# Turning x of a head pair through a scratch in DRAM: four transfers out and one back in place of sixteen

## The chip, the core and the metric

The kernel runs on one core of one Trainium2 chip. The metric is the device time of one execution in microseconds, taken as the median of several runs; beside it there is one profiled execution with a record of the instructions of each engine, of the DMA issues with their landings, and of the clock granted to TensorE (PE).

## The reference

The input is q, k, v of shape (8 batches, 8 heads, 576 positions, 64), all float32, a norm weight g, and the weights of a mixer. The first half is linear attention without a softmax, with an RMS norm over each head's 64 outputs; the second half mixes along the sequence with a rank-32 product and then runs a two-layer network along the channels:

```python
kv = np.einsum('bhsd,bhde->bhse', q, np.einsum('bhsd,bhse->bhde', k, v))   # out
x = out / sqrt(mean(out * out, -1) + 1e-6) * g_norm       # heads side by side: (8, 576, 512)
u = x + (x.transpose(0, 2, 1) @ U @ V).transpose(0, 2, 1)
y = u + np.maximum(u @ w_ch1, 0) @ w_ch2                  # 512 -> 2048 -> 512
```

## The kernel before, in words

**The network.** The 8 x 576 = 4608 positions are cut into nine blocks of 512 columns, j = 0 to 8. The kernel keeps u with channels on the partitions, in two parts (a rounded high part and the rest, so a product takes three matmuls). Blocks 0 and 1 go through all 16 chunks of the hidden size with `ffn1` (L454 to L456, accumulating in the tile h), `relu` (ACT L463 makes hh, DVE L464 makes hl) and `ffn2` (L471, accumulating in y). From block 2 on, `fast_group` takes two chunks at a time by a scheme of seven products instead of eight (L607, into h and pp in turn); DVE and ACT add the products up (L666, L662), make hh and hl (L669, L670), and the matmuls of L625 bring them into y. There are 8 groups a block and 7 such blocks. This is called the fast stage below; it starts at 246 us.

**Weights.** They come as 64-bit words, are decoded on ACT and DVE during block 0, and during block 1 `weight_combos` forms the sums for the seven products on POOL, DVE (L568, L572) and ACT (L570), in tiles named dec and sh. L574 to L577 store them in DRAM tiles wd, one for each of the 8 groups. In the fast stage `load_group` (L597) brings each group's weights back in two loads, wt<-wd, 1024 and 768 KB, into one of two buffer sets; a load waits until PE has finished with the buffer.

**The pairs.** Heads are taken in pairs, four pairs a batch. A pair of batch b is prepared while an earlier block runs: batch 0 before block 0, batch 1 in block 0, batch 2 in block 1, and batches 3 to 7 in the fast stage, so that 28 of the 32 pairs go the way described here and 20 of these in the fast stage. The steps: `kv_step` (PE L274 to L281, after loads of kv_sb and kvt_sb, DVE L272 and L288), `out_step` (PE L300, L302, after the load of q_sb; ACT squares), `stats_step` and `mul_step` (DVE L316 to L331: the norm, giving x with positions on the partitions), `xsplit_step`, `turn_step`, `t_step` and `t4_step` (the rank-32 product), and `mix_part` (PE L440, then DVE L443 adds the turned x). `carry` (ACT L515), `split_cols` and `factor` (L543 to L548) make the network's operands of it.

**The turn.** `turn_step` brings x, positions on the partitions, into ut32[p], channels on the partitions. DVE transposes 32 x 32 squares (L356) into xt; what is left is to move squares between groups of 32 partitions. L359 does it with sixteen transfers, SBUF to SBUF, one for each source group a and target group k, 20 KB each for a = 0 and 1, and 16 KB for a = 2 and 3. The mix of the pair, L443, needs all sixteen.

**The order.** All transfers are issued by SP, one queue, in order; an instruction that waits holds all behind it. SP issues the loads of the pairs and the weights, the turns, the stores of the weight sums and of the output (out<-st, L487). PE's order in the fast stage is written out by hand: the pair steps are put behind numbered products. The order of DVE, ACT, POOL and SP, and PE's in blocks 0 and 1, comes from a scheduler which places each instruction when it takes its operands to be ready; so an instruction's new cost can change the order around it.

Of the kernel before, what the change touches and what calls it, by code (L numbers as in the profile page):

```python
# [10 lines left out]
F32 = mybir.dt.float32  # L11
# [8 lines left out]
B, H, S, D = 8, 8, 576, 64  # L20
DM, DF, R = 512, 2048, 32
P = 128
# [9 lines left out]
QL = [P + 32] * 2 + [P] * 2  # L32
QO = [0, 160, 320, 448]
# [40 lines left out]
def build(ctx: ExitStack, tc: tile.TileContext, kv_in, kvt0_in, kvt_in, q_in, uv_in, g_in, w_in, out):  # L74
    nc = tc.nc
# [14 lines left out]
    ut32 = [ut32_all[:, c, :] for c in range(ND)]  # L90
# [165 lines left out]
    def bank():  # L256
        bank_no[0] += 1
        if startup[0] and bank_no[0] % (7 - NEARLY) >= 3 - NEARLY:
            return ps_y.tile([P, 512], F32, name="y")
        return ps_p.tile([P, 512], F32, name="pp")  # L260
# [73 lines left out]
    def xsplit_step(b, p):  # L334
# [9 lines left out]
        nc.vector.tensor_tensor(out=xh[TAIL:P, 4], in0=s["x"][0:TAIL, 4], in1=xh[0:TAIL, 4].bitcast(F32), op=ALU.subtract)  # L344
        s["hl"] = (xh, xl)

    def turn_step(b, p):

        x = state[b, p]["x"]
        if b == 0:  # L350
            main = state[b, p]["main"] = bank()
            for i in range(4):
                nc.tensor.matmul(main[:, i * P:(i + 1) * P], lhsT=x[:, i, :], rhs=ident, start=(i == 0), stop=False, is_transpose=True)
        else:
            xt = sc.tile([P, 4, NT, 32], F32, name="xt")
            nc.vector.transpose(out=xt.rearrange("p k i j -> p i k j"), in_=x.rearrange("p i (k j) -> p i k j", j=32))  # L356
            for a in range(4):
                for k in range(4):
                    nc.sync.dma_start(out=ut32[p][32 * k:32 * k + 32, QO[a]:QO[a] + QL[a]],  # L359
                                      in_=xt[32 * a:32 * a + 32, k, 0:QL[a] // 32].rearrange("p i j -> p (i j)"))  # L360

    def t_step(b, p):
        tp = bank()
# [414 lines left out]
    def spread_v(n, eng):  # L778
# [4 lines left out]
        out=uv, in_=uvraw.bitcast(U32).rearrange("p (n t) -> p n t", t=2)[:, :, 1].bitcast(F32), func=AF.Abs)  # L783
# [122 lines left out]
    def pair_steps(b, p):  # L906

        nxt = (b, p + 1) if p + 1 < NPAIR else (b + 1, 0)

        def kv():  # L910
            kv_step(b, p)
            if nxt[0] < B:
                load_kv(*nxt)

        def o():
            for what in (out_step, stats_step, mul_step):
                what(b, p)
            if nxt[0] < B:
                load_q(*nxt)

        def t():
            t_step(b, p)
            t4_step(b, p)

        return dict(kv=kv, out=o, carry=lambda: carry(b, p), turn=lambda: turn_step(b, p), xsplit=lambda: xsplit_step(b, p), t=t, mix0=lambda: mix_part(b, p, 0), mix1=lambda: mix_part(b, p, 1))
# [141 lines left out]
```

## Time and profile before

| what | us |
|---|---|
| median of 3 runs | 909.07 (908.11 to 911.46) |
| profiled execution | 908.89 |
| its span | 907.1 |
| PE busy in the span | 888.4 |
| SP: 448 issues of L359, median | 0.588 each |
| DVE at L443 idle for ut<-xt | 17.4, 12 times |

The span runs from the first to the last instruction; 1.79 us of the profiled execution lie around it. A row of a timeline or a group gives, in square brackets, how long the engine stood idle ahead of it and what ended that. A row of SP gives the time in which it issued a number of transfers; the transfers land later.

### The profile page before, as it was taken

The page shows a single profiled execution, that of the slowest core. Times are in us where ns is not written, and L with a number is a line of the kernel's source. Part 1 is how long each engine was busy: PE and PEld are TensorE (multiplying, and loading weights), DVE is VectorE, ACT ScalarE, POOL GpSimd, SP SyncE. Part 2 cuts the span into 40 slices and gives each one's busy share as a digit, 9 for nine tenths or more (in the row PEclk, how much of TensorE's full clock was granted, in tenths as well). Part 3 has the DMA queues.
Part 4 walks back from the last instruction along what each step waited for, and adds up shares of the span by engine and source line. Part 5 has one row for each costly group of instructions (what it writes and reads, how often), then busy time and mean ns, then how long its engine had stood idle before and what let it go on. Part 6 is the DMA issues. An engine that isn't in the chain of part 4 may idle for free.

```text
span 907.1 us, 15333 instructions
## 1 busy us (share of the span) xinstructions
PE 888.4 (98%) x5540; PEld 788.2 (87%) x5540; DVE 569.8 (63%) x1278; ACT 368.3 (41%) x818; POOL 38.0 (4%) x53
## 2 busy tenths in 40 slices
PE   8899999999999999999999999999999999999997
PEld 7678888887889998899999999999999999998997
DVE  5799987668475577566856586558755662253233
ACT  5677743333244353444533354335332432232221
POOL 2000023212010000000000000000000000000000
PEclk9999999999999999999999999999999999999999
DMA  9966355544756565666665557557744665546541
GB/s 345 417 263 195 101 182 158 182 147 155 268 184 243 223 245 166 229 239 216 221 220 224 183 189 257 179 213 259 262 168 174 215 221 186 163 163 213 180 142 47
DMA packets 76541, 186.81 MB, mean 206 GB/s; under 512 B 12721, under 2 KB 45233, under 8 KB 69297
## 3 DMA queue, kind: packets, MB, share of 16 engines
q1 hardware_dynamic: 76464, 185.82, 58.3%
q8 instruction: 44, 0.72, 0.3%
q14 instruction: 33, 0.26, 0.1%
HBM read 149.73 MB, written 24.12 MB: 192 GB/s over the span
## 4 chain that ended last, share of the span: by engine, by line
PE 82%; DMA 7%; DVE 4%; SPq 3%; ACT 2%; issue 1%; POOL 0%; DVEq 0%; ACTq 0%
PE y L625 31%; PE h L607 15%; PE pp L607 14%; PE y L471 6%; SPq L359 3%; PE h L454 2%; PE pp L277 2%; PE h L455 2%; PE pp L300 2%; PE h L456 2%; DMA out<-st 1%; DMA wt<-wd 1%; DMA wd<-dec 1%; DMA ut<-xt 1%; DMA kvq<-kv_in 1%
## 5 line engine op out<-in xcount | busy, mean ns | idle before, releaser
L607 PE MATMUL h<-uc,wt 128*128 128x256 f32 x1176 | 175.2, 285 | 0.3 <-DVE sums L666 0.3
L625 PE MATMUL y<-hh,ws 128*128 128x512 f32 (+1 forms) x528 | 175.1, 389 | 0.0
L607 PE MATMUL pp<-uc,wt 128*128 128x256 f32 x1176 | 173.1, 283 | 0.1
L607 PEld LDWEIGHTS h<-uc,wt 128*128 128x128 f32 x1176 | 161.2, 190 | 10.2 <-DVE sums L666 0.7
L607 PEld LDWEIGHTS pp<-uc,wt 128*128 128x128 f32 x1176 | 154.9, 191 | 0.5 <-DVE sums L666 0.3
L625 PEld LDWEIGHTS y<-hh,ws 128*128 128x128 f32 x528 | 97.5, 189 | 16.2
L625 PE MATMUL y<-dec,ws 128*128 128x512 f32 (+1 forms) x396 | 103.0, 389 | 0.0
L625 PE MATMUL y<-hl,ws 128*128 128x512 f32 (+1 forms) x264 | 102.8, 389 | 0.0
L666 DVE TENSOR_TENSOR sums<-h,dec 128x256 f32<-128x256 f32 x112 | 47.1, 421 | 64.1 <-PE h L607 63.3
L625 PEld LDWEIGHTS y<-dec,ws 128*128 128x128 f32 x396 | 70.3, 189 | 11.9
L669 ACT ACTIVATE hh<-sums 128x512 fp32r<-128x512 f32 x75 | 47.0, 629 | 80.3 <-DVE sums L666 78.7
L666 DVE TENSOR_TENSOR sums<-pp,dec 128x256 f32<-128x256 f32 x112 | 47.1, 421 | 46.0 <-PE pp L607 39.8
L471 PE MATMUL y<-hh,ws 128*128 128x512 f32 x216 | 71.6, 397 | 0.2 <-ACT hh L463 0.2
L662 ACT COPY dec<-h 128x256 f32<-128x256 f32 x84 | 31.2, 372 | 86.2 <-PE h L607 85.9
L670 DVE SCALAR_TENSOR_TENSOR hl<-sums,hh 128x512 fp32r<-128x512 f32 x75 | 51.9, 692 | 18.9 <-ACT hh L669 18.2
L625 PEld LDWEIGHTS y<-hl,ws 128*128 128x128 f32 x264 | 49.9, 189 | 7.6
L454 PE MATMUL h<-ut,ws 128*128 128x512 f32 x112 | 44.9, 401 | 3.3 <-DVE hl L464 3.3
L471 PEld LDWEIGHTS y<-hh,ws 128*128 128x128 f32 x216 | 39.0, 188 | 8.0 <-issue 0.5
L455 PE MATMUL h<-ut,ws 128*128 128x512 f32 x112 | 43.8, 391 | 0.0
L456 PE MATMUL h<-ut,ws 128*128 128x512 f32 x112 | 43.7, 391 | 0.0
L471 PE MATMUL y<-hl,ws 128*128 128x512 f32 x108 | 42.0, 389 | 0.0
L316 DVE TENSOR_REDUCE sums<-x 128x10 f32<-128x640 f32 x28 | 22.9, 817 | 26.9 <-ACT x L304 26.6
(216 smaller groups left out, 1338.0 us busy)
## 6 DMA issues: line engine op xcount, KB each, us to landing
wt<-wd SPq DMA_DIRECT2D x56, 1024.0 KB, 5.8
wt<-wd SPq DMA_DIRECT2D x56, 768.0 KB, 5.2
kv_sb<-kv_in SPq DMA_DIRECT2D x29, 512.0 KB, 5.1
raw<-w_in SPq DMA_DIRECT2D x14, 1023.6 KB, 15.0
out<-st SPq DMA_DIRECT2D x35, 256.0 KB, 5.1
q_sb<-q_in SPq DMA_DIRECT2D x29, 288.0 KB, 5.6
wd<-ws SPq DMA_DIRECT2D x42, 128.0 KB, 3.8
ut<-xt SPq DMA_DIRECT2D x224, 20.0 KB, 2.1
```

The source lines that it names most:

```text
L316: nc.vector.tensor_reduce(out=sums.rearrange("p (i h) -> p i h", h=2), in_=xv, axis=AX.X, op=ALU.add)
L359: nc.sync.dma_start(out=ut32[p][32 * k:32 * k + 32, QO[a]:QO[a] + QL[a]], in_=xt[32 * a:32 * a + 32, k, 0:QL[a] // 32].rearrange("p i j -> ...
L454: nc.tensor.matmul(h, lhsT=w1s[f][0][:, d, :], rhs=uh[d], start=(d == 0), stop=False)
L455: nc.tensor.matmul(h, lhsT=w1s[f][0][:, d, :], rhs=ul[d], start=False, stop=False)
L456: nc.tensor.matmul(h, lhsT=w1s[f][1][:, d, :], rhs=uh[d], start=False, stop=(d == ND - 1))
L471: nc.tensor.matmul(acc, lhsT=w2s[f][w][:, c, :], rhs=h[:, cols], start=(f == 0 and w == 0 and h is hh), stop=(f == NF - 1 and w == 1))
L607: nc.tensor.matmul(acc, lhsT=w[:, ws_, e * P:(e + 1) * P], rhs=u[:, us, e, :], start=fresh and e == 0 and n == 0, stop=e == 1 and n == 2, ...
L625: nc.tensor.matmul(acc, lhsT=w2s[f][w][:, c, :], rhs=h[:, cols], start=start, stop=stop)
L662: return lambda acc: nc.scalar.copy(out=to, in_=acc)
L666: nc.vector.tensor_tensor(out=to, in0=acc, in1=other, op=ALU.add)
L669: nc.scalar.activation(out=hh, in_=sums[:, 1 - i], func=AF.Relu)
L670: nc.vector.scalar_tensor_tensor(out=hl, in0=sums[:, 1 - i], scalar=0.0, in1=hh.bitcast(F32), op0=ALU.max, op1=ALU.subtract)
```

## The change

`turn_step` gets two scratch tiles in DRAM, xds, of 128 x 576 float32, taken in turn by the pairs. The transposed squares xt go there in four stores (after.py L361), one for each source group a of 32 partitions: a store carries all four target groups k, 32 x 4 rows of 640 bytes (64 or 80 KB in all). The fifth transfer (L363) loads the whole scratch, 128 rows of 2304 bytes, 288 KB, into ut32[p]. It reads what the four have written, so SP waits for their landing ahead of it.

```diff
+    xds = [tc.dram_tile([P, S], F32, name=f"xd{i}") for i in range(2)]
+
     def turn_step(b, p):
...
             xt = sc.tile([P, 4, NT, 32], F32, name="xt")
             nc.vector.transpose(out=xt.rearrange("p k i j -> p i k j"), in_=x.rearrange("p i (k j) -> p i k j", j=32))
+            xd = xds[p % 2]
             for a in range(4):
-                for k in range(4):
-                    nc.sync.dma_start(out=ut32[p][32 * k:32 * k + 32, QO[a]:QO[a] + QL[a]],
-                                      in_=xt[32 * a:32 * a + 32, k, 0:QL[a] // 32].rearrange("p i j -> p (i j)"))
+                nc.sync.dma_start(out=xd[:, QO[a]:QO[a] + QL[a]].rearrange("(k j) n -> j k n", k=4),
+                                  in_=xt[32 * a:32 * a + 32, :, 0:QL[a] // 32].rearrange("p k i j -> p k (i j)"))
+            nc.sync.dma_start(out=ut32[p], in_=xd)
```

Lines below the change move by two or three (L443 becomes L446, L597 L600). The change also shifts the numbers of the DRAM tiles: group i of the weight sums is wd_97 + i before and wd_99 + i after.

SP's queue in block 1, at the third pair of batch 2, where the trace shows a turn at 184.96 us and the store wd<-dec behind it at 197.80 us. Before:

```order
L204 DMA q_sb<-q_in 128x576
L359 DMA ut_86<-xt 32x160 x8
L359 DMA ut_86<-xt 32x128 x8
L584 DMA ws_690<-ws_797 128x512 x2
L574 DMA wd_101<-sh 128x4x256
L574 DMA wd_101<-dec 128x4x256
L183 DMA kv_sb<-kv_in 128x1024
```

After, from the stores of the same group's sums (wd_103) on; the turn behind them is that of the second pair of batch 2:

```order
L577 DMA wd_103<-sh 128x4x256
L186 DMA kvt_sb<-kvt_in 128x256
L577 DMA wd_103<-dec 128x4x256
L361 DMA xd_98<-xt 32x4x160 x2
L361 DMA xd_98<-xt 32x4x128 x2
L587 DMA ws_573<-ws_621 128x512
L363 DMA ut_86<-xd_98 128x576
L587 DMA ws_573<-ws_621 128x512
L577 DMA wd_104<-sh 128x4x256
L577 DMA wd_104<-dec 128x4x256
```

The stores of the sums have moved ahead against the turns, by a group or two, and one other transfer stands between the four stores of a turn and its return.

SP's queue in the fast stage, at the pair whose turn begins at 368.59 us in the trace. Before:

```order
L597 DMA wt<-wd_100 128x1536
L359 DMA ut_86<-xt 32x160 x8
L359 DMA ut_86<-xt 32x128 x8
L183 DMA kv_sb<-kv_in 128x1024
L597 DMA wt<-wd_101 128x2048
L597 DMA wt<-wd_101 128x1536
L186 DMA kvt_sb<-kvt_in 128x256
```

After, the same pair:

```order
L600 DMA wt<-wd_102 128x1536
L361 DMA xd_98<-xt 32x4x160 x2
L361 DMA xd_98<-xt 32x4x128 x2
L600 DMA wt<-wd_103 128x2048
L363 DMA ut_86<-xd_98 128x576
L183 DMA kv_sb<-kv_in 128x1024
L186 DMA kvt_sb<-kvt_in 128x256
L600 DMA wt<-wd_103 128x1536
```

The next weight load now stands between the stores and the return; the pair's loads stand behind the return.

## The prediction

> **What bounds the kernel now.** I read the head of the page first, then the busy time by stage, then the waits of PE (TensorE), and only then the timelines at the places where PE waits.
>
> ```profile
> PE 888.4 (98%) x5540; PEld 788.2 (87%) x5540; DVE 569.8 (63%) x1278; ACT 368.3 (41%) x818; POOL 38.0 (4%) x53
> 0.00:40.00 40.00, 34.22 (x210) 28.52 (x211) 25.68 (x71) 21.84 (x55) 6.69 (x29) 1.00 0.96 376
> 40.00:140.00 100.00, 96.23 (x484) 78.78 (x483) 90.76 (x172) 69.02 (x106) 5.13 (x4) 1.00 0.59 198
> 140.00:246.00 106.00, 103.48 (x507) 85.48 (x506) 69.84 (x141) 36.07 (x76) 21.06 (x16) 1.00 0.56 187
> 246.00:900.00 654.00, 652.21 (x4334) 593.70 (x4333) 380.47 (x890) 241.36 (x582) 5.16 (x4) 1.00 0.57 200
> 900.00:907.10 7.10, 2.22 (x13) 1.77 (x11) 3.08 (x5) 0.00 (x0) 0.00 (x0) 0.99 0.41 148
> ```
>
> The rows by stage give the length and then the busy time of PE, weight load, DVE, ACT and POOL, the granted clock (1.00 nearly to the end), the DMA share and GB/s. The change adds and removes no matmul, so it can touch only PE's idle time: 5.78 us in the first 40 us, 3.77 up to 140 us, 2.52 in block 1, 1.79 in the long fast stage from 246 us, 4.88 at the end. Nothing of the changed code runs in the first or the last piece, which leaves 8.08 us, 0.9% of the span. The waits of PE say which part of it has a reason; the first four rows are for 40 to 246 us, the last three for 246 to 900 us (total, times, longest):
>
> ```profile
> PE h L454 <- DVE hl L464: 3.3, 5, 1.4
> PE y L471 <- ACT hh L463: 1.9, 2, 1.6
> PE pp L430 <- DVE x L329: 1.0, 1, 1.0
> PE y L471 <- DVE st L483: 0.2, 1, 0.2
> PE pp L300 <- DVE ut L443: 1.1, 2, 0.9
> PE y L625 <- DVE hl L670: 0.4, 1, 0.4
> PE h L607 <- DVE sums L666: 0.3, 1, 0.3
> ```
>
> PE never waits for a transfer by itself after 40 us. It waits for DVE, and DVE waits for the turned x. The places in the fast stage lie near 361 and 383 us:
>
> ```profile
>   DMA ut<-xt: 17.4, 12
> 368.59 11.53 SPq L359 DMA_DIRECT2D ut<-xt  x16
> 383.11 0.49 DVE L443 TENSOR_TENSOR ut<-pp,ut 128x320 f32<-128x320 f32 x1 [2.72 <-DMA ut<-xt]
> 383.66 1.16 PE L300 MATMUL pp<-kvb,q_sb 128*128 128x128 f32 x8 [0.89 <-DVE ut L443]
> 361.48 1.16 PE L300 MATMUL pp<-kvb,q_sb 128*128 128x128 f32 x8 [0.17 <-DVE ut L443]
> ```
>
> DVE's mix (L443) idled 17.4 us in 12 waits for ut<-xt. At 368.59 the sixteen issues took SP 11.53 us, DVE stood 2.72 us for the last landing, and PE 0.89 us for DVE. In block 1 the turn costs PE in a second way. DVE waits there for a store of the weight sums (wd<-dec, its buffer is reused), and that store stood in SP's queue behind a turn:
>
> ```profile
> 163.88 10.88 SPq L359 DMA_DIRECT2D ut<-xt  x16
> 178.05 0.86 SPq L574 DMA_DIRECT2D wd<-dec  x1
> 183.42 0.76 DVE L568 TENSOR_TENSOR dec<-dec 128x256 f32<-128x256 f32 x2 [2.15 <-DMA wd<-dec]
> 185.56 0.50 PE L454 MATMUL h<-ut,ws 128*128 128x512 f32 x1 [0.49 <-DVE hl L464]
> 184.96 10.82 SPq L359 DMA_DIRECT2D ut<-xt  x16
> 197.80 0.52 SPq L574 DMA_DIRECT2D wd<-dec  x1
> 202.70 0.76 DVE L568 TENSOR_TENSOR dec<-dec 128x256 f32<-128x256 f32 x2 [1.94 <-DMA wd<-dec]
> 204.45 0.50 PE L454 MATMUL h<-ut,ws 128*128 128x512 f32 x1 [0.26 <-DVE hl L464]
> 211.60 0.50 PE L454 MATMUL h<-ut,ws 128*128 128x512 f32 x1 [1.40 <-DVE hl L464]
>   DMA wd<-dec: 5.6, 4
> ```
>
> Twice the same: a turn of almost 11 us on SP, the store late, DVE held for about 2 us, hl late, PE idle; the last row is DVE's whole waiting time for these stores. So 0.17 + 0.89 = 1.06 us in the fast stage and 0.49 + 0.26 + 1.40 = 2.15 us in block 1 hang on the turn, 3.2 us together.
>
> **The change part by part.** The rows for its prices: issue time on SP (min/median/max ns) and time from issue to landing (min/median/max us) of today's turn, of the stores of L574, wd<-sh and its like, which have the new store's three-dimensional form, of the load q_sb, which has the new return's size, shape and direction. Then the smallest store, the sizes of the other two with their median landing, and SP's waits for PE.
>
> ```profile
> L359 SPq DMA_DIRECT2D ut<-xt x448: 507/588/1921, 58.6 to 707.4; - x150
> DMA to landing us min/median/max: 1.7/1.8/7.0
> L574 SPq DMA_DIRECT2D wd<-sh x8: 371/396/561, 130.7 to 233.9; - x8
> DMA to landing us min/median/max: 3.2/4.3/6.0
> L204 SPq DMA_DIRECT2D q_sb<-q_in x29: 328/333/1072, 1.6 to 668.3; - x29
> DMA to landing us min/median/max: 2.9/5.7/11.2
> out<-st SPq DMA_DIRECT2D x2, 128.0 KB, 1.7
> wd<-sh SPq DMA_DIRECT2D x8, 512.0 KB, 3.8
> q_sb<-q_in SPq DMA_DIRECT2D x29, 288.0 KB, 5.6
> SPq L597 <- PE pp L607: 101.7, 38, 6.0
> SPq L597 <- PE h L607: 92.3, 34, 6.3
> ```
>
> Removed: sixteen issues a turn, 16 x 0.588 = 9.4 us and in the timeline 10.8 to 11.5 us with the waits between them. With the 1.8 us of the last landing a turn takes 12.6 to 13.3 us from its first issue, 14.5 where DVE waited until 383.11; I take 12.6.
>
> Added: four issues. Their form is nearest to wd<-sh, so 4 x 0.40 = 1.6 us (bounds 0.37 and 0.56 each). The fourth starts 1.2 us after the first and lands after 1.7 us by the smallest store and after 3.2 us by the fastest of L574, which are six to eight times larger; each new store is 64 or 80 KB, so I take the middle, 2.4 us, and have the data in DRAM at 3.6 us. Bounds: 1.7 us, and 6.0 us by the slowest of L574. Then SP issues the return, which lands after 2.9, 5.7 or 11.2 us; with a weight load mostly just ahead of it in the rings I take 5.7. Sum 1.2 + 2.4 + 5.7 = 9.3 us, that is 3.3 us earlier than today. Best case 1.2 + 1.7 + 2.9 = 5.8; worst 1.7 + 6.0 + 11.2 = 18.9.
>
> The added wait is SP's: the return may not issue before the four stores have landed, and everything behind it in SP's queue (in the fast stage the next kv, kvt, q and weight loads) stands for those 2.4 us. SP is still free after about 4 us where it was busy for 11, so those loads go earlier and not later; PE waited for none of them after 40 us when they stood behind sixteen issues. In the fast stage a weight load (L597 by the old numbering) often stands between the stores and the return and itself waits until PE has freed its buffer. These waits were 101.7 + 92.3 us in 72, 2.7 us each; they run beside the 2.4 us of the stores' landing, so they add 0.3 us on average, and 6.3 at most.
>
> By rows, then, the sum is 9.3 to 9.6 us and the two waits of DVE that PE felt, near 361 and 383 us, go: -1.06 us. Against this speaks a rule. The fastest loads of q_sb landed after 2.9 us and the median after 5.7, so a trip through DRAM does stretch under load here. The Trainium skill (DMA: Bandwidth & Descriptors, Latency and other measured facts) puts an access to HBM at 0.2 us on average and 2 us at high load; as an estimate from that page, two loaded trips in a row would add 4 us to the turn, 13.3 us instead of 9.3, and nothing would be gained. No row here shows a store of 64 KB followed by its own reading back, so I keep this as a rival.
>
> In block 1 the instructions also stand in another order: the order of DVE, ACT and of PE's pair steps is the scheduler's, and it differs from the first pair steps of that block on. The stores wd<-dec stand ahead of the turn now or behind five short issues. If both DVE waits go, 2.15 us come back; since other waits may come with the new order (bounds: all 2.15 gained; as much lost), I take half, -1.1 us.
>
> One wait of PE lies ahead of the first issue of a turn at 58.6 us, as the 1.0 us at L430 does, and stays:
>
> ```profile
> 54.51 0.50 PE L454 MATMUL h<-ut,ws 128*128 128x512 f32 x1 [0.92 <-DVE hl L464]
> ```
>
> Costed at nothing: the DVE transpose and the mix itself, which stay; 28 x 288 KB more written to DRAM and read back, because the DMA share is 0.57 on average and the same 288 KB a turn no longer go from SBUF to SBUF.
>
> Sum: 1.06 + 1.1 = 2.1 us (2.16 before rounding) off the profiled execution's 908.89 us (span 907.1) gives 906.8; the median of the runs shown, 909.07, is 0.18 above that execution, so I predict **907.0 us**.
>
> **The rivals.**
> *The two DRAM trips eat the saving.* Stores at the median of L574, 4.3, the weight load's wait of 2.7 not beside them, the return at 5.7: 1.2 + 4.3 + 2.7 + 5.7 = 13.9 us, today's length. For it speaks that DMA is 57% busy; against it the small size of the stores. The 1.06 us stay, block 1 may go either way: 909.1 us, 908.4 to 910.5.
> *Slower: DVE is held longer at the mix.* The place is L443 in the fast stage, where DVE stands in order in front of the sums that PE needs (L666). Today 17.4 us of DVE's waits made 1.06 us of PE's, 0.06 per us, but near 383 us it was 0.89 for 2.72, a third. With twenty turns in that stage it takes 4.5 / (20 x 0.33) = 0.7 us more than today for each turn, a turn over 13.3 us, for a loss of 0.5%; at 3 us more, 15.6 us, and 0.2 per us, the loss is 12 us: 921 us. A turn of 13.3 us needs returns at 9.7 us as a rule, or at 7.8 behind stores at 4.3, against a median of 5.7.
> *Block 1's new order loses a little*: two more waits of the 1.40 us kind, 911.5 us.
> *Faster by more:* of the 8.08 us of idle time, 6.2 lie after the first turn. If DVE's and ACT's backlog dissolves as well, 5 of these go: 904 us. Against it: most of the rest has reasons that the turn doesn't touch (ACT hh, st).
> That the change doesn't do what it says can be set aside: SP's new order has four stores and one load per pair.
>
> **How the numbers follow.** Chances: the forecast (905.5 to 908.4) 0.50, trips eat it 0.27, held longer 0.12, new order loses 0.05, faster by more 0.06. About 0.5%, 4.5 us, is what a measurement of this kernel can tell from no change; the forecast, the eaten saving and the small loss lie within it: same 0.82, faster 0.06, slower 0.12. A range from 904.4 to 912.5 us holds these three and leaves the 921 and the 904 us cases out.
>
> **What would show it.** Right: L443 waits for ut<-xd under 5 us in all instead of 17.4; SP busy with a turn for 4 to 5 us; the return's landing near 6 us; DVE's waits for wd<-dec at L568 (5.6 us today) at most half; PE idle in 246 to 900 us near 0.7 us and in block 1 near 1.4. Wrong: a turn over 13 us from first issue to landing, L443 waiting more than today, PE waiting at L300 or L607 for DVE in many turns, or a PE wait for kv_sb or wt behind the blocked queue.

## The result, and the profile after

The changed kernel took 915.4 us (median of 4 runs, 914.51 to 916.36) against 908.86 us of the kernel before in the same job (908.11 to 911.46): a ratio of 1.0067, 95% interval 1.0043 to 1.0091. By the ratio it is slower by 6.1 us, by the two medians by 6.5 us, where 907.0 us was forecast and the range ended at 912.5. The profiled execution took 914.51 us with a span of 912.7.

First the busy time by stage of the changed kernel, with the columns and four of the five stages of the table in the prediction (length, PE, weight load, DVE, ACT, POOL, granted clock, DMA share, GB/s):

```profile
0.00:40.00 40.00, 33.04 (x210) 27.50 (x210) 25.75 (x71) 21.69 (x55) 6.67 (x29) 1.00 0.95 372
40.00:140.00 100.00, 95.43 (x481) 78.39 (x479) 91.64 (x174) 69.21 (x106) 5.27 (x4) 1.00 0.64 213
140.00:246.00 106.00, 98.78 (x471) 80.53 (x472) 68.31 (x137) 34.61 (x73) 21.64 (x16) 0.98 0.58 187
246.00:900.00 654.00, 653.05 (x4336) 595.00 (x4335) 379.84 (x890) 241.94 (x583) 5.15 (x4) 1.00 0.66 211
```

PE idles 7.22 us in the third stage, where it idled 2.52, and 0.95 us in the fast stage, where it idled 1.79. The extra 1.18 us in the first stage is no loss: PE has issued 210 matmuls by 40 us in both. Stages cut at fixed times hide how far a kernel has got, so I also read two fixed points of the program from the timelines, ACT's last relu of block 0 and PE's first product of the fast stage, before and after:

```profile
143.03 0.59 ACT L463 ACTIVATE hh<-h 128x512 fp32r<-128x512 f32 x1
244.45 0.88 PE L607 MATMUL h<-uc,wt 128*128 128x256 f32 x6
```

```profile
143.53 0.60 ACT L466 ACTIVATE hh<-h 128x512 fp32r<-128x512 f32 x1 [0.64 <-PE h L459]
251.58 0.64 PE L610 MATMUL h<-uc,wt 128*128 128x256 f32 x4
```

From the one to the other it is 101.4 us before and 108.1 us after: block 1 alone is 6.6 us longer. What comes ahead of it differs by 0.5 us, and the fast stage up to the end of the span takes 661.1 us instead of 662.7.

The waits of PE in 40 to 246 us, the two large ones of block 1, and two of DVE for transfers over the whole span (total, times, longest; line numbers from L361 on are 3 higher than before, those of the turn apart):

```profile
PE h L457 <- DVE hl L467: 6.3, 7, 2.3
PE y L474 <- DVE st L486: 2.9, 1, 2.9
...
DVE dec L571 <- DMA wd<-dec: 8.1, 4, 3.2
DVE x L446 <- DMA ut<-xd: 8.0, 6, 3.3
```

PE still waits above all for DVE. ACT's hh keeps it for 1.6 us, 1.9 before, and there is no wait for kv_sb or wt. The wait of DVE for the stores of the weight sums has not shrunk from 5.6 us, it has grown to 8.1.

The place of the largest loss is near 152 us. DVE's timeline, and below it PE's row, after; then DVE at the same place before:

```profile
149.58 0.76 DVE L571 TENSOR_TENSOR dec<-dec 128x256 f32<-128x256 f32 x2 [3.19 <-DMA wd<-dec]
152.72 1.23 DVE L575 TENSOR_TENSOR dec<-dec,sh 128x1024 fp32r<-128x1024 f32 x1 [1.15 <-ACT sh L573]
153.87 0.68 DVE L486 TENSOR_TENSOR st<-y,ut 128x512 f32<-128x512 f32 x1
...
154.70 0.76 PE L474 MATMUL y<-hh,w2s 128*128 128x512 f32 x1 [2.91 <-DVE st L486]
```

```profile
148.95 0.69 DVE L483 TENSOR_TENSOR st<-y,ut 128x512 f32<-128x512 f32 x1 [3.00 <-PE y L471]
...
152.63 1.84 DVE L568 TENSOR_TENSOR dec<-dec 128x256 f32<-128x256 f32 x3 [1.20 <-DMA wd<-dec]
154.39 0.55 DVE L443 TENSOR_TENSOR x<-pp,ut 128x384 f32<-128x384 f32 x1
```

Before, DVE made the output sums st of block 0 as soon as PE had them, and then the weight sums of group 2. After, these weight sums (L571 and L575) stand ahead of st. They wait 3.19 us for a store and 1.15 us for ACT, and st, on which PE's next accumulation waits, comes 4.9 us later. Before, the store that DVE waits for here was issued at 148.01 us, behind twelve transfers of the turn, and landed 4.5 us later, while DVE made the output sums. After, no turn stands in front of it: it is issued at 144.18 us and lands after 5.3 us, but DVE now wants its buffer sooner.

The gap has a tail. The two rows are the gap and the 3.5 us behind it, with the columns of the table by stage: PE's busy time stands behind the comma, the granted clock behind the five busy times.

```profile
151.80:154.60 2.80, 0.00 (x0) 0.00 (x0) 1.88 (x3) 1.39 (x2) 0.52 (x1) 0.95 0.35 120
154.70:158.20 3.50, 3.50 (x9) 2.67 (x10) 2.56 (x5) 0.00 (x0) 3.50 (x4) 0.57 0.59 196
```

At a granted clock of 0.57 those 3.5 us cost 1.5 us (3.5 x 0.43) more. So this one place takes 4.4 of the 6.6 us.

The second place is the turn of pair (2,0), the first in block 1. In order: SP issues its four stores, ACT carries, SP issues the return, DVE mixes, and PE stands for an hl that DVE makes only behind the delayed steps of the next pair.

```profile
139.22 1.77 SPq L361 DMA_DIRECT2D xd<-xt  x4
162.46 0.90 ACT L518 COPY x<-ut 128x128 f32<-128x128 f32 x4
163.08 0.43 SPq L363 DMA_DIRECT2D ut<-xd  x1
167.09 0.56 DVE L446 TENSOR_TENSOR x<-pp,ut 128x384 f32<-128x384 f32 x1 [3.27 <-DMA ut<-xd]
178.92 0.50 PE L457 MATMUL h<-ut,ws 128*128 128x512 f32 x1 [2.26 <-DVE hl L467]
```

The data was in DRAM by 142.3 us, and the return came 20.8 us later. It overwrites all 576 columns of the tile at once, and ACT's carry (L518) still has to copy the last 128 of them; in the kernel before the carry ran at 152.30 us, when POOL's part of block 0's output sums was done. Those sums are late now (POOL is through with the third at 160.7 us), and ACT makes an sh of the weight sums, at 161.51 us, ahead of the carry. Before, only the last four of the sixteen transfers overwrote those columns; the first twelve went at once.

The turn itself, in the two lines of SP that issue it: issue time in ns, then the time to landing in us (minimum, median, maximum).

```profile
L361 SPq DMA_DIRECT2D xd<-xt x112: 318/432/1926, 59.5 to 706.2; - x112
DMA to landing us min/median/max: 1.7/2.7/6.3
...
L363 SPq DMA_DIRECT2D ut<-xd x28: 320/338/1184, 69.5 to 708.0; - x28
DMA to landing us min/median/max: 2.7/3.8/5.4
```

In the twenty turns of the fast stage it is 7.2 to 10.4 us from the first issue to the return's landing, with a median of 8.8 us, where 9.3 was forecast. Two turns ahead of that stage are far longer: the first of all takes 13.6 us, since a dozen other transfers stand in SP's queue between its stores and its return, and pair (2,0) takes 27.8 us.

### The profile page after: what moved, and what is told of

Its sections match the earlier page's. It is cut to its first block, busy times and chain, and to the rows that moved or that the text cites. A ratio compares the mean times of both kernels' runs of the same rounds, so it can differ in the third digit from the quotient of the medians.

```text
span 912.7 us, 14823 instructions
## 1 busy us (share of the span) xinstructions
PE 888.3 (97%) x5540; PEld 788.4 (86%) x5540; DVE 570.8 (63%) x1278; ACT 368.7 (40%) x818; POOL 38.7 (4%) x53
## 4 chain that ended last, share of the span: by engine, by line
PE 83%; DVE 8%; DMA 5%; ACT 2%; issue 1%; SPq 0%; DVEq 0%; ACTq 0%
PE y L628 33%; PE pp L610 15%; PE h L610 15%; PE y L474 5%; DMA wd<-dec 2%; PE pp L277 2%; PE pp L300 2%; PE h L457 2%; PE h L458 2%; PE h L459 2%; DVE dec L571 1%; DMA kvq<-kv_in 1%; PE pp L373 1%; DMA out<-st 1%; PE pp L443 1%
```

## The experiments

The theories. **A:** the loss is the new order of block 1, above all on DVE, with the late return of pair (2,0). **B:** the trips through DRAM cost, by traffic or landing times, wherever they are made. **C:** part of it lies in the first 40 us. All ratios are against the kernel before in the same job, with a 95% interval; "block 1" is the time between the two fixed points above in the one profile of each run.

| run | ratio (interval) | median us | block 1 us |
|---|---|---|---|
| before | | 908.9 to 910.7 | 101.4 |
| after | 1.0067 (1.0043 to 1.0091) | 915.4 | 108.1 |
| e1 scratch only in the fast stage | 0.9983 (0.9971 to 0.9994) | 907.45 | 100.7 |
| e2 two returns | 1.0057 (1.0041 to 1.0073) | 914.29 | 108.9 |
| e3 group 2's sums later | 1.0021 (1.0010 to 1.0032) | 910.90 | 103.8 |
| e4 both | 1.0016 (1.0004 to 1.0028) | 910.94 | 104.4 |
| e5 scratch, old order | 0.9971 (0.9958 to 0.9983) | 906.67 | 99.9 |
| e6 the same, two returns | 0.9955 (0.9941 to 0.9969) | 905.00 | 98.4 |
| e7 sixteen transfers, new order | 1.0379 (1.0360 to 1.0399) | 943.66 | 120.9 |
| e8 two trips more | 1.1175 (1.1139 to 1.1211) | 1016.43 | 101.0 |
| e9 scratch, only DVE's old order | 0.9955 (0.9941 to 0.9969) | 906.20 | 99.7 |
| e10 after, again | 1.0052 (1.0037 to 1.0066) | 915.81 | 108.8 |
| e11 two trips more, order free | 1.1099 (1.1070 to 1.1128) | 1011.18 | 101.1 |
| e12 one trip more | 1.0388 (1.0353 to 1.0423) | 945.71 | 101.1 |

**e1: the scratch only where PE's order is fixed.**

```diff
+            if b > FAST:
                 xd = xds[p % 2]
                 for a in range(4):
                     nc.sync.dma_start(out=xd[...], in_=xt[...])
                 nc.sync.dma_start(out=ut32[p], in_=xd)
+            else:
+                for a in range(4):
+                    for k in range(4):
+                        nc.sync.dma_start(out=ut32[p][32 * k:32 * k + 32, ...], in_=xt[32 * a:32 * a + 32, k, ...])
```

> Batches 1 and 2, whose turns run before 246 us, turn x with the sixteen transfers from SBUF to SBUF; the twenty turns of the fast stage go through the scratch. Theory A (the loss lies in block 1, in the order of the instructions there): the orders of DVE, ACT and PE up to 246 us are those of before, so block 1 has before's idle time of PE (2.5 us) and the fast stage keeps what it gained in the changed kernel (0.95 us idle instead of 1.79): about 908.0 us against 908.9, a ratio of 0.999, within 0.998 to 1.001. Theory B (the trips through DRAM cost, by traffic or by landing times, wherever they are made): 20 of the 28 turns still make them, so 20/28 of the 6.5 us stay, 913 us, a ratio of 1.005. Theory C (part of the loss is in the first 40 us, where PE idled 1.18 us more, and comes with the scratch existing): 909.2 us.

Measured 907.45 us, 0.9983 (0.9971 to 0.9994), as theory A has it. Block 1 and the fast stage of this run:

```profile
140.00:246.00 106.00, 103.84 (x510) 86.03 (x509) 70.36 (x142) 36.48 (x77) 21.27 (x16) 1.00 0.56 187
246.00:900.00 654.00, 653.34 (x4342) 595.23 (x4341) 381.80 (x893) 241.18 (x581) 5.15 (x4) 1.00 0.65 209
```

Block 1 idles 2.16 us again, the fast stage 0.66. Twenty of the 28 turns go through DRAM and the kernel is faster: theory B falls, since it wanted 913 us. Theory C falls too: PE idles 6.38 us in the first 40 us here as well, and the time shows nothing of it; in the changed kernel's second profile (e10) it idles only 5.24 us there, and the loss is the same.

**e2, e3 and e4: the two places apart and together.** e2 splits the return for batches 1 and 2 at the column from which ACT's carry reads; e3 holds DVE's weight sums of group 2 behind the third output sum; e4 has both.

```diff
-            nc.sync.dma_start(out=ut32[p], in_=xd)
+            for part in (slice(0, QO[3]), slice(QO[3], S)) if b <= FAST else (slice(0, S),):
+                nc.sync.dma_start(out=ut32[p][:, part], in_=xd[:, part])
```

```diff
-            nc.vector.tensor_tensor(out=o, in0=acc, in1=uh[c].bitcast(F32), op=ALU.add)
+            added = nc.vector.tensor_tensor(out=o, in0=acc, in1=uh[c].bitcast(F32), op=ALU.add)
+            if c == 2:
+                last["st"] = added
...
-                weight_combos(f // 2)
+                with tc.issue_after(last["st"].ins) if f // 2 == 2 else ExitStack():
+                    weight_combos(f // 2)
```

> The changed kernel, but in batches 1 and 2 the return comes in two transfers, columns 0 to 447 and 448 to 575, so that only the second, which overwrites what ACT's carry copies (L518), has to wait for these copies; the order of DVE keeps the weight sums of group 2 ahead of the sums st of block 0's output, but for 24 rows it is the changed kernel's. Theory A: the first piece of pair (2,0) is issued at about 143 us instead of 163, DVE's 3.3 us wait for ut<-xd goes, and so does most of PE's gap of 2.26 us near 176 us, while the gap of 2.9 us near 152 us stays: 912 to 913.5 us, a ratio of 1.004. Theory B: nothing changes but one transfer more for each of eight turns: 915.4 us, 1.007. If the late return is the whole cause: 908 to 909.5 us.

Measured 914.29 us, 1.0057 (1.0041 to 1.0073): within error of the changed kernel, and above theory A's 912 to 913.5. SP did issue the first piece early, but little came of it:

```profile
140.99 0.34 SPq L364 DMA_DIRECT2D ut<-xd  x1
```

```profile
150.36 0.42 PE L444 MATMUL pp<-v,t 128*128 128x384 f32 x2
```

```profile
160.73 0.55 DVE L447 TENSOR_TENSOR x<-pp,ut 128x384 f32<-128x384 f32 x1
```

The first piece had landed at 144.3 us and PE's product for the mix (L444) was there at 150.8, but DVE's order had changed little, and the mix (L447) ran at 160.73 us: without a wait and 6.4 us earlier than in the changed kernel, yet still behind weight sums and output sums that it doesn't need. The gap at st stayed, at 2.68 us. The one of 2.26 us became one of 1.19, and a later one grew to 1.93. In this order the late return is not what costs, and the second half of theory A as I had put it falls.

> The changed kernel, but DVE's weight sums of group 2 in block 1 are queued behind the third of the four sums st of block 0's output; the return stays one transfer. Theory A: the gap of 2.9 us near 152 us goes, POOL's second sums and with them ACT's carry come about 5 us earlier, the return follows them, so part of the 2.26 us near 176 us goes as well: 910 to 912 us, a ratio of 1.002. Theory B: 915.4 us, 1.007. If the late return alone were the cause: 914 us.

Measured 910.90 us, 1.0021 (1.0010 to 1.0032): in the expected span, about 4 us better than the changed kernel by one change on DVE. The output sums are back at their time, right when PE has them, and the gap of 2.9 us is gone:

```profile
150.72 0.69 DVE L486 TENSOR_TENSOR st<-y,ut 128x512 f32<-128x512 f32 x1 [3.18 <-PE y L474]
...
187.93 0.51 PE L457 MATMUL h<-ut,ws 128*128 128x512 f32 x1 [2.18 <-DVE hl L467]
```

The second row shows what stays: a gap of 2.18 us behind an hl that stands late in DVE's queue.

> Both edits at once: two returns in batches 1 and 2, and group 2's weight sums behind the output sums of block 0. DVE's order near 150 us is then that of before again. Theory A: both gaps go, block 1 idles about 2 to 3 us on PE, the fast stage keeps its gain: 907.5 to 909.5 us, a ratio of 0.9985 to 1.001. Theory B: 914 to 915.4 us, 1.006. Theory C: up to 1.2 us above theory A's value.

Measured 910.94 us, 1.0016 (1.0004 to 1.0028), that is 909.6 to 911.8 us, where 907.5 to 909.5 was expected. Two edits don't bring the old order back: the scheduler put other steps elsewhere, and PE waited 1.93 us near 186 us for ACT's xh, a gap that neither kernel had. So the order had to be held as a whole.

**e5, e6 and e9: the scratch in the order of before.** The order of the kernel before, as ranks of each engine's instructions, is written into the changed kernel, and each instruction is queued behind its old neighbour (issue order only, no wait is added between engines).

```diff
+HELD = dict(DVE='...', Activation='...', PE='...')
...
+    for name, text in HELD.items():
+        own = [i for i in traced if str(i.engine).split(".")[-1] == name]
+        order = [int(r.split("+")[0]) + k for r in text.split() for k in range(int((r + "+1").split("+")[1]))]
+        for a, b in zip(order, order[1:]):
+            if free[a] and free[b]:
+                tc.add_manual_dep(own[b], own[a].name, mybir.DependencyInfo(mybir.DependencyClass.NoSync, mybir.DependencyReason.DATA), reason="held")
```

> The changed kernel, all 28 turns through the scratch with one return each, but the instructions of DVE (the first 420), ACT (400) and PE (1000, all of block 0's rest and block 1) are held in the order in which they stand in the kernel before. Theory A (the loss is the new order of block 1, with the late return that goes with it): group 2's weight sums stand behind the output sums again and ACT's carry behind its old neighbours, so the return of pair (2,0) comes near 156 us instead of 163: the gaps of 2.9 and 2.26 us go, DVE's mix of (2,0) waits some 2 to 4 us longer than in the kernel before, and the fast stage gains 1 us: 908 to 910 us, a ratio of 0.999 to 1.001. Theory B (the trips through DRAM): 915 us, 1.0067, whatever the order.

Measured 906.67 us, 0.9971 (0.9958 to 0.9983), better than the 908 to 910 expected. All 28 turns use the scratch, and the loss is gone:

```profile
140.00:246.00 106.00, 104.45 (x515) 86.71 (x514) 71.96 (x145) 36.15 (x78) 21.07 (x16) 1.00 0.61 198
```

PE idles 1.55 us in that stage. The return of (2,0) is still late here, at 154.60 us, and costs one gap of 0.99 us.

> As the run with the old order, and with two returns for each turn of batches 1 and 2, so that the first 448 columns don't wait for ACT's carry. Theory A: nothing of the new order and nothing of the late return is left, so the time is that of the run in which only the fast stage uses the scratch, 907.5 us, or up to 1 us less by block 1's shorter turns: 906.5 to 908, a ratio of 0.997 to 0.999. Theory B: 915 us, 1.0067.

Measured 905.00 us, 0.9955 (0.9941 to 0.9969), the best of all with e9. SP issues the first piece at 140.63 us, DVE mixes at its old place without any wait, and block 1 idles 0.57 us:

```profile
140.63 0.34 SPq L372 DMA_DIRECT2D ut<-xd  x1
...
153.34 0.55 DVE L455 TENSOR_TENSOR x<-pp,ut 128x384 f32<-128x384 f32 x1
```

```profile
140.00:246.00 106.00, 105.43 (x531) 88.42 (x530) 72.35 (x143) 37.12 (x79) 23.49 (x18) 1.00 0.61 198
```

Here, in the old order, splitting the return is worth 1.5 us of block 1 (99.9 to 98.4 us); in the times of the whole kernel the intervals of e5 and e6 overlap.

> The changed kernel with one return for each turn, and only DVE's first 420 instructions held in the order of the kernel before; ACT and PE stand as the scheduler then puts them. If it is DVE's order that costs (theory A in its narrow form: DVE's queue, with the weight sums ahead of the output sums and of hl), the time is that of the run with all three orders held: 906.7 us, within 905.5 to 908.5, a ratio of 0.996 to 0.999. If the orders of ACT and PE in block 1 carry half of the loss: 910 to 911 us, 1.001 to 1.002.

Measured 906.20 us, 0.9955 (0.9941 to 0.9969); the changed kernel in the same job 915.81 us, 1.0052. Holding DVE's first 420 instructions alone takes away the loss:

```profile
140.00:246.00 106.00, 104.50 (x516) 86.78 (x516) 72.58 (x146) 36.47 (x78) 21.10 (x16) 1.00 0.61 198
```

So DVE's order is enough. It is not shown that the new orders of ACT and PE would cost nothing by themselves, since they weren't kept: with DVE held the scheduler put ACT and PE nearly as before. ACT's carry, for one, runs at 154.54 us ahead of the sh of group 2 at 158.98 (152.30 and 155.30 before), where in the changed kernel that sh comes at 151.65 and the carry at 162.46. Of DVE's order, e3 names a part that is worth some 4 of the 9.6 us between the changed kernel and this one; which other rows make up the rest was not tried.

**e7: the mirror image.** The kernel before, its sixteen transfers kept, with the ranks of the changed kernel written in (the same code).

> The mirror image: the kernel before with its sixteen transfers from SBUF to SBUF and no scratch, but with the instructions of DVE (the first 420), ACT (400) and PE (1000) held in the order in which they stand in the changed kernel. Theory A: it pays for the order without any trip through DRAM: 912 to 915 us, a ratio of 1.003 to 1.0067 (the late return is not there, so it may stay below the changed kernel's time by the 0.9 us that two returns gave, and the fast stage keeps before's 1.8 us of idle time). Theory B: 909 us, 1.000.

Measured 943.66 us, 1.0379 (1.0360 to 1.0399), far above both expectations. It is not the clean mirror that I took it for. The new order leaves room for a turn that frees SP at once, and this one doesn't:

```profile
100.71 10.01 SPq L367 DMA_DIRECT2D ut<-xt  x16
110.82 0.53 SPq L191 DMA_DIRECT2D kv_sb<-kv_in  x1
111.44 0.38 SPq L194 DMA_DIRECT2D kvt_sb<-kvt_in  x1
...
115.16 0.40 ACT L279 CAST tails<-kvt_sb 128x256 fp32r<-128x256 f32 x1 [8.61 <-DMA kvt_sb<-kvt_in]
```

The load kvt_sb stands behind ten us of issues, ACT's tails wait 8.61 us for it ahead of the hh that PE needs, and PE stands for 7.6 us. That an order costs without any DRAM trip is shown; how much of the changed kernel's 6.1 us it would be is not, and e5, e6 and e9 answer that instead.

**e8, e11 and e12: how long may a turn be?** In the fast stage of e1's kernel the scratch is copied to a second one in DRAM (e12), or to a second and a third (e8, e11), before it is read back; DVE and ACT are held in e1's order, but not in e11.

```diff
-                nc.sync.dma_start(out=ut32[p], in_=xd)
+                nc.sync.dma_start(out=xcs[0][p % 2], in_=xd)
+                nc.sync.dma_start(out=xcs[1][p % 2], in_=xcs[0][p % 2])
+                nc.sync.dma_start(out=ut32[p], in_=xcs[1][p % 2])
```

> As the run in which only the fast stage's twenty turns use the scratch (907.5 us), with the orders of DVE and ACT held as there, but each of these turns makes two more trips: the scratch is copied to a second and a third one in DRAM before it is read back, all issued by SP. The turn should take 15 to 18 us instead of 8.6, longer than the 12.6 us of the kernel before. By the prediction's rival of a DVE that is held at the mix, a turn of 15.6 us loses 12 us against the kernel before: 920 us or more, a ratio of 1.012. If the turn's length is off the path that PE feels up to far more than that, and only the few places count at which PE waited before: 909 to 912 us, 1.000 to 1.003.

> The kernel with two more trips through DRAM in each turn of the fast stage, but DVE and ACT ordered by the scheduler, which knows of the longer turn, instead of held in the order for the short one. If the held order was to blame for 1016 us (DVE stood 123 us at the mix while it had other work): 915 to 940 us. If a turn of 16 us is too long for PE's hand-written order, in which the mix has a fixed place: 990 to 1020 us.

> As the run with the long turn and held orders, but with one more trip instead of two: the turn should take 12 us, between 8.6 (907.5 us) and 15.7 (1016 us). At 15.7 us DVE stood 6.2 us at the mix in each of twenty turns and PE 3.8 us for it, so PE has some 2.4 us of slack behind DVE. By that slack DVE stands some 2.5 us a turn and PE 0.3 us: 912 to 920 us, a ratio of 1.003 to 1.012. If the cost goes in proportion to the turn's length: 109 us x 3.4 / 7.1 = 52 us more, 960 us, 1.056.

Measured 1016.43, 1011.18 and 945.71 us, with median turns of 15.7, 15.7 and 12.9 us. The waits in the fast stage, of e8 first, then of e12:

```profile
DVE x L462 <- DMA ut<-xc: 123.2, 20, 8.8
...
PE pp L459 <- DVE x L462: 75.8, 19, 7.3
```

```profile
DVE x L461 <- DMA ut<-xc: 62.9, 18, 6.3
...
PE pp L458 <- DVE x L461: 28.4, 13, 5.1
```

1016 us is far above both figures given for e8, the loss of 12 us and the 909 to 912 us, and e12 lies between its two (912 to 920 and 960); e11 came out as a turn too long for PE's order. The held order was not to blame: with the order free (e11) DVE stood 80.5 us instead of 123.2, but PE stood 74.0 us all the same, since its own order is written by hand. The extra times, 109 us for e8 and 38 us for e12 over e1's 907.45, are larger than PE's waits. The rest goes with the clock: over the profiled execution it is 0.956 in e8 and 0.987 in e12, against 0.999 in e1. Gap and tail of e8 near 270 us:

```profile
269.70:276.50 6.80, 0.00 (x0) 0.00 (x0) 0.49 (x2) 0.00 (x1) 0.00 (x0) 0.78 0.49 170
276.60:280.00 3.40, 3.40 (x15) 3.30 (x16) 1.86 (x5) 1.59 (x4) 0.00 (x0) 0.50 0.00 0
```

So turns of 8.8 us cost this stage nothing that shows (e1), and turns of 12.9 us cost 4%; where between the two the limit lies was not tried. Why could the kernel before live with 12.6 us? Its DVE rows for the first turn of the fast stage (first issue at 260.52 us) show it:

```profile
269.20 0.49 DVE L443 TENSOR_TENSOR x<-pp,ut 128x320 f32<-128x320 f32 x1
272.66 0.42 DVE L443 TENSOR_TENSOR ut<-pp,ut 128x256 f32<-128x256 f32 x1
```

So it isn't the whole mix that needs all sixteen transfers, as the description of the turn has it. Its first half reads 320 columns and needs only the first eight, the last of which had landed at 266.7 us, 6.2 us after the first issue; only the second half needs the sixteenth, which landed at 272.4. Neither waits here; in e12 the first half of the same turn stands 5.97 us. One return lands all columns together. So the turn got 3 us shorter for the second half and 2.6 us longer for the first. This reading of the two traces was not tested by a kernel of its own.

**e10: the changed kernel again.**

> The changed kernel once more, on the chip of these runs. If the loss is the order's and no accident of one execution, its profile shows PE's gap near 152 us (2.9 us) behind the output sums and the one near 176 us (2.3 us) behind hl again, each within 0.5 us, a granted clock under 0.7 for some 3.5 us behind the first, and a time of 914.5 to 916.5 us, a ratio of 1.005 to 1.008.

Measured 915.81 us, 1.0052 (1.0037 to 1.0066). Both gaps are there, of 3.12 and 2.22 us, and behind each the clock is low:

```profile
156.40:159.90 3.50, 3.47 (x8) 2.54 (x9) 2.56 (x5) 0.00 (x0) 3.50 (x4) 0.59 0.58 195
...
180.70:184.10 3.40, 3.40 (x9) 2.62 (x10) 3.02 (x7) 0.63 (x3) 0.00 (x0) 0.53 0.32 70
```

## Why the prediction was wrong

**The bound.** PE bounds both kernels, and its busy time is the same (888.4 and 888.3 us). But that "it can touch only PE's idle time" was incomplete: the matmuls behind a gap can run at a lower granted clock (0.57 for 3.5 us here), so the gap of 2.91 us cost 4.4.

**The turn.** Right in its length as a rule, 8.8 us (9.3 forecast): 0.43 us an issue (0.40), 2.7 us for the stores (2.4), 3.8 us for the return (5.7). The sum came that near by luck, because two errors offset each other: the return landed 1.9 us sooner, but it was issued 4.7 us after the first store in the median of the fast stage, where 3.6 to 3.9 was forecast. Two of the 28 turns took more than the 13 us that were named as a sign of being wrong. The rival of two DRAM trips that eat the saving didn't come. Its sentence on the Trainium skill (DMA: Bandwidth & Descriptors, Latency and other measured facts) made 13.3 us of it, as an estimate, by adding 2 us of loaded latency to each trip; the fast stage's longest turn was 10.4 us. A wait was missed: the return may overwrite the tile only when ACT's carry has read it, 20.8 us late in pair (2,0). By e2 that costs nothing in the new order that could be measured, and by e5 and e6 some 1.5 us of block 1 in the old one.

**The fast stage, -1.06 us.** Right in direction and size as far as it can be measured: e1 gives -1.6 us (-2.6 to -0.5). The two gaps at L300 are gone, but others of 0.2 to 0.5 us come and go: PE's idle time there is 0.66 to 2.29 us in eight profiles of kernels whose fast stage uses the scratch (after, e1 to e5, e9, e10; e6 ends early, and its 3.13 us hold part of the end) against 1.79 in before's one profile, so a single profile could not have shown the gain.

**Block 1, where it failed.** The step was: "If both DVE waits go, 2.15 us come back; since other waits may come with the new order (bounds: all 2.15 gained; as much lost), I take half, -1.1 us." Block 1 lost 6.6 us. The order of DVE was known to change, and I bounded what it could cost by the size of what it could give. Nothing joins the two. A changed order can put any wait ahead of any step, and what it costs is set by what stands behind it: here the output sums st, without which PE can't reuse its accumulator. The bound on the gain holds for this change: with the scratch and DVE's old order block 1 is 1.5 and 1.7 us shorter (e5, e9; 3.0 us with the return split as well, e6). The bound on the loss doesn't. The rival "block 1's new order loses a little" had the mechanism, at "two more waits of the 1.40 us kind" and a chance of 0.05; the waits were 2.9 and 2.3 us, and the first brought 1.5 us of low clock.

**DVE held longer at the mix.** It didn't happen to this change: DVE waits 8.0 us for the turn instead of 17.4 (under 5 forecast), 3.3 of them at the late return. As a price it was much too low: 12 us for a turn of 15.6 us, where e8 measured 109 us for 15.7. The slope came from two places at which PE had waited, and left out the slack used up at all others, the clock, and that one return makes the first half of the mix wait as long as the second.

**SP's new wait.** Harmless, as forecast: the wait for the stores held up no load that PE waited for.

## What to carry to other kernels

Where a scheduler decides the order, a change of a transfer is two changes, and the order must be compared and priced by what now stands in front of each step that the bounding engine waits for; the time saved says nothing about that price. To tell the two apart, hold the old order on the engine that the bound waits for: here that turned a loss of 0.5% into a gain of 0.45%, with the transfers unchanged. When many small transfers become one, look for readers that needed only the first of them, and for a reader that now holds up the whole.

## What the runs showed of the hardware

A gap in PE's work can be paid for twice. Behind gaps of 2.9 to 6.8 us PE ran for about 3.4 us at a granted clock of 0.50 to 0.59 and then at 0.92 to 1.00 (e8, e10 and the changed kernel); behind one of 5.08 us in e12 it was some 5.3 us at 0.50. The Trainium skill (TensorE: Matmul & The Clock Gate, Part 1: The HAM clock gate (the "warmup" mystery)) has half clock after an idle window of some 3.4 us, until a busy one of the same length. The 3.4 us at 0.50 agree; the gap needed was shorter here: 2.9 us was enough, one of 2.22 us was followed by 0.53 in e10, and the same gap, of 2.26 us, in the first profile of the changed kernel by 1.00:

```profile
179.00:182.50 3.50, 3.50 (x16) 2.87 (x17) 3.00 (x7) 0.73 (x3) 0.00 (x0) 1.00 0.26 57
```

The length of a gap doesn't decide it alone. Near 52 and 54 us, ahead of the first turn, PE has two gaps of 0.9 to 1.0 us in every profile. In four of the fourteen (e3, e5, e9, e10) the clock was at 0.50 for some 3 us behind the second, in the others not; e5 first, then the kernel before:

```profile
55.00:58.00 3.00, 3.00 (x7) 2.38 (x8) 2.93 (x6) 1.18 (x2) 0.00 (x0) 0.50 1.01 382
```

```profile
55.00:58.00 3.00, 3.00 (x15) 2.47 (x14) 2.93 (x6) 1.49 (x2) 0.00 (x0) 1.00 1.01 376
```

In these four the last relu of block 0 starts at 144.0 to 145.3 us, in the others, e7 apart, at 142.1 to 143.5. So some 2 us between two executions can come from a place ahead of the first turn; the times of block 1 hold none of it.
